# Turning the memory rows with 16 identity columns, partly in 64-wide tiles

## The chip, the cores and the metric

The program runs on one core of a Trainium2 chip. The metric is the device time of one execution in microseconds (us); three executions of the kernel before took 1811.97, 1812.57 and 1812.88 us, so the median is 1812.57. One more execution was taken with the hardware profiler, and every duration below comes from it.

## The reference

The operator joins two independent parts along the last axis. Part A is a long convolution (a shift filter, a product with `v`, an FFT convolution over 2048 positions, a skip term and a product with `q`). Part B is a transformer layer that carries eight memory rows from segment to segment; the change lies in part B:

```python
mem = mem0                                             # 8 rows of 1024
for s in range(n_seg):                                 # 64 segments of 32 rows
    h = concat([mem, x[:, 32*s:32*s+32]], axis=1)      # 40 rows
    q, k, v = (einsum('btd,dhe->bhte', h, W) for W in (Wq, Wk, Wv))   # 32 heads of 128
    p = softmax(where(mask, einsum('bhqe,bhke->bhqk', q, k) * scale, -1e9))
    o = einsum('bhte,hed->btd', einsum('bhqk,bhke->bhqe', p, v), Wo)
    mem = o[:, :8]
    outs.append(o[:, 8:])
```

A segment needs the first eight output rows of the one before it, so the segments follow one another strictly. The weights are bfloat16, 1024 x 4096 for each of q, k and v and 4096 x 1024 for the output.

## The kernel before

The first 437 us or so hold part A and, woven into it, the work of part B that doesn't depend on the memory (the last eight rows of every segment are projected there, and the `x` rows are stored transposed in `REC`). Then come the 64 segments, one after another, in an order written out by hand (`tc.manual_schedule`): each engine runs the instructions in the order of the code, and the framework adds the waits.

**Weights.** The weights are cut into chunks of 128 x 2048 bfloat16 (512 KB). Most stay in SBUF for all segments under names such as `Wres`, `Wmid`, `Wlate`, `Wmore` and `pw`; two are held in spare PSUM columns and copied out in quarters (`quarter`, `quarter_b`; a part of one lies in the second half of `tps`). The other chunks, 14 in a segment, are read again in every segment from a DRAM copy `WS` into `wring`, a ring of five tiles. `fetch()` issues such a load on SP's queue as soon as `done()` has released a tile, that is, when the last matmul that reads it is through.

**A segment.** `rec` is loaded by a POOL DMA; its first 256 columns are `hT`, the segment's input transposed: eight blocks of 128 input features by 32 rows, of which columns 0 to 7 are the memory rows and 8 to 31 `x` rows. `Proj.run` (L941) multiplies one block of `hT`, a 128 x 32 stationary operand, with a chunk: four matmuls, one for each 32 columns of the array (`tile_position=(0, 32 * c)`), each with 512 moving columns. The order of the projections is k0, q0, k1, q1, v0, v1, with transposes, scores, softmax and attention between them. The output projection (`out_half`, L1032) has the attention output as a stationary operand 64 columns wide, so two matmuls of 256 moving columns stand side by side (`tile_position=(0, 64 * dh)`). It accumulates the output features in four quarters, two for each `yacc[f]`, f = 0 and 1. ScalarE copies `yacc[f]` to `Y` (L1121): rows 0 to 39 hold the 40 output rows for the features of the first half, rows 64 to 103 those of the second half.

**The memory rows.** `fill_mem(hT, Y, half)` brings the eight memory rows from `Y` into columns 0 to 7 of the next segment's `hT`. For each of its two 128-column blocks of `Y`, `turn_tile` (L885) transposes the block in four matmuls with the identity as the moving operand (128 columns, `is_transpose`), each writing 32 rows of the bfloat16 PSUM tile `tps`. Then one VectorE copy (L894) takes the wanted 32 values of each partition, 8 of every 64 columns, to `hT`. `turn_tile` also serves the transposes of k0 and q0, which don't change.

**Where it is called.** Half 0 needs only the features of `yacc[0]`. It is called inside the output projection of f = 1, before the fourth of its five last chunks (L1113 and L1114), so that its copy runs beside the chunks that follow. Half 1 needs `yacc[1]`; it is called in the next segment after the first four steps of k0 (L1055), followed by two steps of q0 and then by the steps of k0 that read it. The first segment calls both on `mem0` (L1052, L1055); the last one doesn't call half 0.

Of the kernel before, what the change touches and what calls it, by code (L numbers as in the profile page):

```python
# [10 lines left out]
F32 = mybir.dt.float32  # L11
# [411 lines left out]
def b_kernel(ctx: ExitStack, tc, x, mem0, Wq, Wk, Wv, Wo, outb, n_seg, run_a):  # L423
    nc = tc.nc
    SEG = 32
    NX = 24
    NM = 8
# [47 lines left out]
    ident = const.tile([128, 128], BF, name="ident")  # L475
# [263 lines left out]
    with c0p:  # L739
# [16 lines left out]
        for g in range(2):  # L756
# [3 lines left out]
            for tb in range(4):  # L760
                vst = vsts[:, tb] if g == 0 else pair()[:].rearrange("p (c w) -> p c w", c=4)
                for c in range(4):
                    ps = ps0.tile([128, 512], F32, tag="ps0", name="vb_ps")
                    for kc in range(8):
                        v_last = nc.tensor.matmul(ps[:], lhsT=xbt(kc)[:, 16 * tb:16 * tb + 16, :].rearrange("p s t -> p (s t)"),  # L765
                                                  rhs=ws[kc][:, c * 512:(c + 1) * 512], start=(kc == 0), stop=(kc == 7))
# [21 lines left out]
    tps = ps_t.tile([128, 2, 512], BF, name="tps")  # L788
# [89 lines left out]
    pend = {}  # L878
# [6 lines left out]
    def turn_tile(dst, src):  # L885
        for e in range(0, 128, 32):
            nc.tensor.matmul(dst[e:e + 32, :], lhsT=src[:, e:e + 32], rhs=ident[:], start=True, stop=True,  # L887
                             is_transpose=True, tile_position=(0, e))

    def fill_mem(hT, Y, half):  # L890
        tp = tps[:, 0, :]
        for j in (2 * half, 2 * half + 1):
            turn_tile(tp[:, j * 128:(j + 1) * 128], Y[:, j * 128:(j + 1) * 128])
        nc.vector.tensor_copy(  # L894
            hT.rearrange("p (dh j) t -> p dh j t", dh=2)[:, :, 2 * half:2 * half + 2, 0:NM],
            tp.rearrange("p (j dh r) -> p dh j r", j=4, dh=2)[:, :, 2 * half:2 * half + 2, 0:NM])

    with tc.manual_schedule():
        for _ in range(RING - 2):
# [2 lines left out]
        Y = one.tile([128, 512], BF, tag="PT", name="Y0")  # L902
# [3 lines left out]
        with tc.issue_after(v_last.ins):  # L906
            nc.tensor.matmul(SB[:, 0:320], lhsT=ident[:], rhs=P_pad[:].rearrange("p b k -> p (b k)"), start=True, stop=True,
                             skip_group_check=True)
# [7 lines left out]
        for s in range(n_seg):  # L916
            now[0] = s
            last = s + 1 == n_seg
            hT, KBs, QBs = pend.pop(s)
# [116 lines left out]
            def out_half(hp, f, OT, stop=False):  # L1036
                w = pieces((3, hp, 0))
                for hh in range(2):
                    project(2 * hp + hh, f, w, OT, stop and hh == 1)
                if f == 1:  # L1040
                    done((3, hp, 0))
# [6 lines left out]
            def out_quarter(ch, q, w):  # L1048
                project(2 * ch[1] + q // 2, q % 2, w, OT1)

            if s == 0:
                fill_mem(hT, Y, 0)  # L1052
            k0 = Proj(0, 0).run(4)
            q0 = Proj(1, 0)
            fill_mem(hT, Y, 1)  # L1055
            q0.run(2)
            k0 = k0.run(4).evac()
# [52 lines left out]
            Y = one.tile([128, 512], BF, tag="PT", name="Y")  # L1110
            for f, hps in enumerate((LAST, LAST[-1:] + LAST[:-1])):
                for n, hp in enumerate(hps):
                    if f == 1 and n == 3 and not last:  # L1113
                        fill_mem(pend[s + 1][0], Y, 0)  # L1114
                    out_half(hp, f, OT1, n == 4)
                    for step in steps.get((f, n), ()):
                        if len(step) == 2:
                            out_quarter(KEPT_A if step[0] == "A" else KEPT_B, step[1], qs.pop(step))
                        else:
                            qs[step[:2]] = (quarter if step[0] == "A" else quarter_b)(*step[1:])  # L1120
                nc.scalar.copy(Y[:, 256 * f:256 * f + 256], yacc[f][:, 0:256])  # L1121
# [6 lines left out]
def kernel(  # L1128
# [27 lines left out]
    with ExitStack() as ctx_b:  # L1156
        b_kernel(ctx_b, tc, B_x[0], B_mem0[0],
                 B_Wq.rearrange("d h e -> d (h e)"), B_Wk.rearrange("d h e -> d (h e)"),
                 B_Wv.rearrange("d h e -> d (h e)"), B_Wo.rearrange("h e d -> (h e) d"),
                 outb, n_seg, run_a)  # L1160
# [35 lines left out]
```

## Time and profile before

| | |
|---|---|
| median of three executions | 1812.57 us |
| the profiled execution | 1807.46 us |
| its span, first to last instruction | 1805.7 us |
| TensorE (PE) busy | 1700.6 us, 94% |
| weight loads (PEld) busy | 999.9 us, 55% |
| VectorE (DVE) busy | 1035.2 us, 57% |
| ScalarE (ACT) busy | 658.6 us, 36% |
| HBM traffic | 344 GB/s over the span |

The span is the time from the first to the last instruction that the profiler saw; the execution's own time is 1.8 us longer. A row of a timeline gives the start in us, the duration, the engine, the line, the operation and its tiles (`out<-in`), and how many instructions were joined (x8 is eight). TensorE's matmuls overlap: four matmuls on different 32-column tiles run side by side, and a matmul's duration includes its way through the array, so what a group of matmuls costs is read from start to start and not from durations. A row of the chain of work is start, time on the chain, and the engine with its line. In a group's row the numbers after the bar are busy us, mean ns of one instruction, and idle us of the engine just before them with what ended it. In the view of waits a row is total us, number of waits and the longest.

### The profile page before, as it was taken

The numbers are of one execution on the slowest core, as the hardware profiler recorded it, in microseconds if no ns is written. First come the engines' busy times: TensorE is split into PE (matmuls) and PEld (weight loads), VectorE is DVE, ScalarE is ACT, GpSimd is POOL, SyncE is SP. The second block draws the span as 40 slices with busy tenths as digits, with TensorE's granted clock in tenths as the row PEclk, the third lists the DMA queues.
The fourth block names the chain that finished last, engine by engine and source line by source line (L and its number), as shares of the span: only waits on it lengthen the run. The fifth ranks groups of instructions, "written<-read, shape, count | busy, mean of one in ns | idle before, by whom it ended". The sixth has DMA issues, their size and how long they took to land.

```text
span 1805.7 us, 71361 instructions
## 1 busy us (share of the span) xinstructions
PE 1700.6 (94%) x30996; PEld 999.9 (55%) x31028; DVE 1035.2 (57%) x3429; ACT 658.6 (36%) x1157; POOL 266.1 (15%) x499
## 2 busy tenths in 40 slices
PE   6889997697899999999999999999999999999998
PEld 3443333243566666666666666666666656666665
DVE  9926885433455555555556555555555555555555
ACT  6954650001233333333333333333333333333333
POOL 4002342100111111111111111111111111111111
PEclk9999998799999999999999999999999999999999
DMA  9989988999999999999999999999999999999997
GB/s 344 358 316 293 307 276 274 317 314 309 335 353 367 356 360 351 360 361 361 363 353 365 358 358 370 361 356 358 362 351 363 364 347 363 363 363 364 357 364 294
DMA packets 233071, 623.35 MB, mean 345 GB/s; under 512 B 72802, under 2 KB 72946, under 8 KB 232756
## 3 DMA queue, kind: packets, MB, share of 16 engines
q1 hardware_dynamic: 160948, 550.58, 82.8%
q0 software_dynamic: 17056, 45.13, 7.1%
q10 hardware_dynamic: 54752, 23.07, 4.8%
q8 instruction: 243, 3.98, 0.9%
q14 instruction: 72, 0.59, 0.1%
HBM read 563.63 MB, written 57.67 MB: 344 GB/s over the span
## 4 chain that ended last, share of the span: by engine, by line
PE 76%; DMA 10%; DVE 7%; ACT 4%; issue 3%; ACTq 1%; POOL 0%; SPq 0%; POOLq 0%; DVEq 0%
PE acc L941 32%; PE yacc L1032 23%; DMA wring<-WS 5%; PE kb_ps L624 4%; PE tps L887 3%; PE vb_ps L765 2%; PE tps L960 2%; ACT OT L1022 2%; DVE mx L975 2%; DVE E L977 2%; PE s_ps L247 1%; DMA REC<-stage 1%; DMA out_dram<-ot 1%; ACT s_sb L249 1%; PE ks_ps L285 1%
## 5 line engine op out<-in xcount | busy, mean ns | idle before, releaser
L1032 PEld LDWEIGHTS <-OT 128*64 128x64 bf16 x8255 | 439.3, 109 | 58.4 <-ACT OT L1022 37.1
L941 PEld LDWEIGHTS <-rec 128*32 128x32 bf16 x12288 | 288.4, 96 | 266.6 <-DVE rec L894 36.5
L950 ACT CAST qkv_sb<-acc 128x512 bf16<-128x512 f32 x384 | 225.1, 586 | 511.7 <-PE acc L941 506.0
L941 PE MATMUL acc<-Wres,rec 128*32 128x512 bf16 x3328 | 238.8, 380 | 1.8 <-issue 1.8
L941 PE MATMUL acc<-wring,rec 128*32 128x512 bf16 x2300 | 226.9, 381 | 6.6 <-DMA wring<-WS 5.5
L1032 PE MATMUL yacc<-Wmore,OT 128*64 128x256 bf16 (+1 forms) x2560 | 220.1, 274 | 0.0
L941 PE MATMUL acc<-Wmid,rec 128*32 128x512 bf16 x3072 | 211.7, 379 | 1.7 <-issue 1.7
L1032 PE MATMUL yacc<-wring,OT 128*64 128x256 bf16 x2448 | 195.9, 274 | 6.6 <-DMA wring<-WS 6.6
L1121 ACT CAST Y<-yacc 128x256 bf16<-128x256 f32 x128 | 47.7, 373 | 274.1 <-DVE quarter_b L797 168.1
L941 PE MATMUL acc<-pw,rec 128*32 128x512 bf16 x1796 | 142.9, 380 | 1.1 <-issue 1.0
L797 DVE TENSOR_SCALAR quarter<-OTp 128x256 int32<-128x256 int32 x252 | 99.6, 416 | 73.2 <-ACT OT L1022 73.2
L1022 ACT CAST OT<-OTp 128x640 bf16<-128x640 f32 x128 | 87.5, 683 | 138.3 <-PE OTp L1014 138.2
L1123 POOL DMA_DIRECT2D out_dram<-Y x128 | 63.7, 502 | 499.9 <-ACT Y L1121 499.8
L894 DVE COPY rec<-tps 128x32 bf16<-128x32 bf16 x128 | 22.3, 174 | 173.5 <-PE tps L887 173.5
L941 PE MATMUL acc<-Wlate,rec 128*32 128x512 bf16 x1536 | 116.7, 379 | 0.2 <-issue 0.2
L1060 DVE COPY KT<-tps 128x512 bf16<-128x512 bf16 x64 | 27.2, 425 | 152.6 <-PE tps L887 152.6
L975 DVE TENSOR_REDUCE mx<-SB 128x8 f32<-128x320 f32 x128 | 62.9, 492 | 71.0 <-PE SB L969 71.0
L882 POOL DMA_DIRECT2D rec<-REC x64 | 36.3, 567 | 443.9 <-PE acc L941 428.3
L980 ACT ACTIVATE E<-E 128x320 f32<-128x320 f32 x128 | 60.1, 469 | 77.8 <-DVE E L977 77.8
L1032 PE MATMUL yacc<-Wlate,OT 128*64 128x256 bf16 x1024 | 78.8, 276 | 6.0
L624 PE MATMUL kb_ps<-XBT,pw 128*128 128x512 bf16 x314 | 80.6, 394 | 2.5 <-DMA pw<-in_B_Wk_dram 1.4
L925 POOL COPY KT<-rec 128x128 bf16<-128x128 bf16 x128 | 38.4, 300 | 261.6 <-PE SB L969 257.6
(222 smaller groups left out, 2629.4 us busy)
## 6 DMA issues: line engine op xcount, KB each, us to landing
wring<-WS SPq DMA_DIRECT2D x831, 512.0 KB, 6.0
wring<-WS SPq DMA_DIRECT2D x64, 384.0 KB, 5.3
rec<-REC POOLq DMA_DIRECT2D x64, 192.0 KB, 5.6
SK<-s_sb SPq DMA_DIRECT2D x16, 512.0 KB, 5.3
SU<-s_sb SPq DMA_DIRECT2D x16, 512.0 KB, 4.9
Kg<-SK SPq DMA_DIRECT2D x32, 256.0 KB, 4.1
Ug<-SU SPq DMA_DIRECT2D x32, 256.0 KB, 5.4
REC<-stage ACTq DMA_DIRECT2D x16, 512.0 KB, 13.3
```

Source lines behind the costliest of these rows:

```text
L624: nc.tensor.matmul(ps[:], lhsT=ws[kc][:, hl * 128:(hl + 1) * 128], rhs=xbt(kc).rearrange("p s t -> p (s t)"), start=(kc == 0), stop=(kc == 7))
L797: nc.vector.tensor_scalar(out=dst, in0=src, scalar1=0, scalar2=None, op0=ALU.bitwise_or)
L887: nc.tensor.matmul(dst[e:e + 32, :], lhsT=src[:, e:e + 32], rhs=ident[:], start=True, stop=True, is_transpose=True, tile_position=(0, e))
L925: nc.gpsimd.tensor_copy(KT[:, :, :, 32:40], KBs[:, 128 * g:128 * g + 128].rearrange("p (c i t) -> p i c t", c=4, i=4))
L941: nc.tensor.matmul(self.acc[32 * c:32 * c + 32, :], lhsT=hT[:, ch[1], :], rhs=w[:, 512 * c:512 * c + 512], start=(ch == chs[0]), stop=(ch ...
L950: nc.scalar.copy(sb[:], self.acc[:])
L975: nc.vector.tensor_reduce(out=mx[:], in_=S, op=ALU.max, axis=AX.X)
L980: nc.scalar.activation(E[:], E[:], ACT.Exp, scale=scale)
L1022: nc.scalar.copy(OT[:], o_view)
L1032: nc.tensor.matmul(yacc[f][64 * dh:64 * dh + m, x - o:y - o], lhsT=lhsT, rhs=r, start=(h == (0, 2 * FIRST[-1])[f] and x == o), stop=stop, ...
L1121: nc.scalar.copy(Y[:, 256 * f:256 * f + 256], yacc[f][:, 0:256])
L1123: nc.gpsimd.dma_start(bass.AP(outb.tensor, outb.offset + SEG * s * 2048 + 512 * dh, [[2048, 32], [1, 512]]), Y[64 * dh + NM:64 * dh + 40, :])
```

## The change

The turned rows are computed by ordinary matmuls with float32 output in place of transposes. The moving operand is no longer the whole identity but `mem_cols`, its columns 0 to 7 and 64 to 71, so a matmul has 16 moving columns and yields just the eight memory rows of both feature halves. The output lies in the first 64 float32 columns of what was the transposes' half of `tps`; half 0 uses columns 0 to 31 and half 1 columns 32 to 63. The copy reads contiguous float32 in place of every eighth stretch of bfloat16. `fill_mem` gets a width: 32 as before, in two rounds of four matmuls, or 64, in two rounds of two. The call inside the output projection passes 64; the calls beside the projections keep 32. Over the program TensorE gets 252 fewer matmuls and 252 fewer weight loads; the orders of the other engines and the waits are the same.

```diff
-    def fill_mem(hT, Y, half):
-        tp = tps[:, 0, :]
+    mem_cols = ident[:].rearrange("p (dh x) -> p dh x", dh=2)[:, :, 0:NM]
+
+    def fill_mem(hT, Y, half, wide=32):
+        tp = tps[:, 0, 0:128].bitcast(F32)
         for j in (2 * half, 2 * half + 1):
-            turn_tile(tp[:, j * 128:(j + 1) * 128], Y[:, j * 128:(j + 1) * 128])
+            for e in range(0, 128, wide):
+                nc.tensor.matmul(tp[e:e + wide, 16 * j:16 * j + 16], lhsT=Y[:, j * 128 + e:j * 128 + e + wide], rhs=mem_cols,
+                                 start=True, stop=True, skip_group_check=True, tile_position=(0, e))
         nc.vector.tensor_copy(
             hT.rearrange("p (dh j) t -> p dh j t", dh=2)[:, :, 2 * half:2 * half + 2, 0:NM],
-            tp.rearrange("p (j dh r) -> p dh j r", j=4, dh=2)[:, :, 2 * half:2 * half + 2, 0:NM])
+            tp.rearrange("p (j dh r) -> p dh j r", j=4, dh=2)[:, :, 2 * half:2 * half + 2, :])
...
-                        fill_mem(pend[s + 1][0], Y, 0)
+                        fill_mem(pend[s + 1][0], Y, 0, 64)
```

## The prediction

> **What bounds the kernel now.** I read the page first, then the windows of the steady part, the chain of work, the DMA view, the waits, and last the instructions around the two places that the change touches. From the page, what the DMAs moved in its forty slices of 45 us (the 64 segments begin in the tenth):
>
> ```profile
> GB/s 344 358 316 293 307 276 274 317 314 309 335 353 367 356 360 351 360 361 361 363 353 365 358 358 370 361 356 358 362 351 363 364 347 363 363 363 364 357 364 294
> ```
>
> Windows of the part with the 64 segments (us, PE, PEld, DVE, ACT, POOL busy; then granted clock, DMA share, GB/s):
>
> ```profile
> 900.00:1000.00 100.00, 98.44 (x2134) 62.87 (x2129) 58.63 (x222) 36.06 (x67) 11.63 (x26) 1.00 0.98 358
> ...
> 1600.00:1700.00 100.00, 99.47 (x2193) 63.97 (x2185) 57.40 (x221) 35.92 (x67) 13.15 (x29) 1.00 0.99 365
> ```
>
> TensorE is busy 98 to 99% at the full granted clock, and the 16 DMA engines are busy 98 to 99% in the same windows. Two resources are full at once, so the question is which one sets the length of a segment. The chain shows one `tps` group of eight matmuls of 0.23 us per segment (`fill_mem` inside the output projection); their starts are a clock for the segments:
>
> ```profile
> 512.16 0.23 PE tps L887 x8
> ...
> 1591.34 0.23 PE tps L887 x8
> 1612.19 0.23 PE tps L887 x8
> ...
> 1695.55 0.23 PE tps L887 x8
> ...
> 1758.56 0.23 PE tps L887 x8
> ```
>
> The five segments from 1591.34 to 1695.55 take 104.21 / 5 = 20.84 us each, and so does 1591.34 to 1612.19. That is the floor that TensorE sets when nothing makes it wait. Not all are so short. The first and last row enclose 59 segments: 1246.40 / 59 = 21.13 us on average, 0.29 us over the floor, 16.8 us in all. Counted by the starts of the 60 VectorE copies that follow these fills, 25 of the 59 lie within 0.03 us of the floor. What ends the extra time, in the waits of the steady part:
>
> ```profile
> PEld L941 <- issue: 17.9, 31, 1.3
> ...
> PE acc L941 <- DMA wring<-WS: 3.8, 8, 0.9
> ```
>
> The second row names the streamed weights. The first has no named releaser, but it stands before the same projections and its 31 waits of 0.58 us on average have the size of the segments' excess; I read it as the same cause. The DMA view of the steady part shows how close the stream is:
>
> ```profile
> DMA packets 132006, 460.39 MB, mean 360 GB/s; under 512 B 17419, under 2 KB 17419, under 8 KB 131733
> ```
>
> ```profile
> wring<-WS SPq DMA_DIRECT2D x788, 512.0 KB, 6.0
> wring<-WS SPq DMA_DIRECT2D x60, 384.0 KB, 5.3
> ```
>
> 848 loads in 1280 us are one in 1.51 us, each 6.0 us under way: 6.0 / 1.51 = 4.0 of the ring's five tiles are in flight at any time. TensorE has about one loaded tile in hand. So it is the nominal bound, with the weight stream right behind it.
>
> **The change part by part.** The place in the output projection (`fill_mem(..., 0)`) and the place after the first four projection steps (`fill_mem(..., 1)`), TensorE's starts in a floor segment:
>
> ```profile
> 1653.37 0.39 PE L1032 MATMUL yacc<-Wmore,OT 128*64 128x256 bf16 x4
> 1653.59 0.27 PE L1032 MATMUL yacc<-B_rest,OT 128*64 128x256 bf16 x2
> 1653.65 0.22 PE L1032 MATMUL yacc<-quarter_b,OT 128*64 128x128 bf16 x1
> 1653.80 0.29 PE L887 MATMUL tps<-ident,Y 128*32 128x128 bf16 x8
> 1654.03 0.41 PE L1032 MATMUL yacc<-Wring,OT 128*64 128x256 bf16 x4
> 1654.27 0.39 PE L1032 MATMUL yacc<-pw,OT 128*64 128x256 bf16 x4
> 1654.58 0.40 PE L941 MATMUL acc<-wring,rec 128*32 128x512 bf16 x4
> 1654.81 0.82 PE L941 MATMUL acc<-Wlate,rec 128*32 128x512 bf16 x12
> 1655.46 0.28 PE L887 MATMUL tps<-ident,Y 128*32 128x128 bf16 x8
> 1655.57 0.60 PE L941 MATMUL acc<-Wmid,rec 128*32 128x512 bf16 x8
> 1656.02 0.40 PE L941 MATMUL acc<-wring,rec 128*32 128x512 bf16 x4
> ```
>
> *Half 0, in the output projection.* From the start of the `quarter_b` matmul to that of `pw` pass 1654.27 - 1653.65 = 0.62 us. Without the fill these would be a half-width step (1653.59 to 1653.65, 0.06) and four `Wring` matmuls (as 1653.37 to 1653.59, 0.22): 0.28. The fill costs 0.34 us, three times the 0.11 that the same eight matmuls cost at 1655.46, where the neighbours are 32 columns wide as they are. The difference stands in the gaps to 64-wide neighbours: 1653.71 to 1653.80 before it, and as much after it. The change removes both switches and leaves four 64-wide matmuls of 16 moving columns, two rounds of two.
>
> *Price of a round.* No row of before has 16 columns. The nearest is the score matmul with 40, four tiles side by side:
>
> ```profile
> 1660.49 0.27 PE L966 MATMUL SB<-KT,QT 128*32 128x40 bf16 x16
> 1660.59 0.24 PE L969 MATMUL SB<-KT,rec 128*32 128x160 bf16 x4
> ```
>
> Sixteen in 0.10 us, with their sixteen weight loads, are 0.025 a round; 1660.59 is rounded, so I take 0.027. The upper end is the 64-wide round as it runs now, 0.22 / 2 = 0.11, in which the loads are hidden behind 256 columns. I take 0.027, since both are rounds of few columns, and keep 0.11 for the range. Half 0 then costs 0.054 in place of 0.34: 0.286 saved, at worst 0.12. Times 63 segments: 18.0 us (7.6).
>
> *Half 1, beside the projections.* Two rounds of 0.027 in place of the 0.11 between 1655.46 and 1655.57: 0.056 saved, at worst nothing. Times 64: 3.6 us (0). The call ahead of the first segment happens once and counts nothing.
>
> The Trainium skill ("TensorE: Matmul & The Clock Gate", LDWEIGHTS) lets a weight load take its columns over 1.2 per ns, so by an estimate from it 64 columns take 53 ns and a half-0 round 0.053 us; half 0 would then save 0.234, and the predicted time below would be 1805.1. The 0.025 of the 32-wide rounds fits that rule; no row of before shows 64-wide loads without cover.
>
> *The copies.* Both fills end in a VectorE copy, now out of float32 PSUM:
>
> ```profile
> L894 DVE COPY rec<-tps 128x32 bf16<-128x32 bf16 x128 | 22.3, 174 | 173.5 <-PE tps L887 173.5
> L1060 DVE COPY KT<-tps 128x512 bf16<-128x512 bf16 x64 | 27.2, 425 | 152.6 <-PE tps L887 152.6
> L975 DVE TENSOR_REDUCE mx<-SB 128x8 f32<-128x320 f32 x128 | 62.9, 492 | 71.0 <-PE SB L969 71.0
> L966 PE MATMUL SB<-KT,QT 128*32 128x40 bf16 x2048 | 35.2, 180 | 1.1 <-issue 1.1
> ```
>
> ```profile
> 1654.20 0.17 DVE L894 COPY rec<-tps 128x32 bf16<-128x32 bf16 x1 [1.27 <-PE tps L887]
> 1655.79 0.17 DVE L894 COPY rec<-tps 128x32 bf16<-128x32 bf16 x1 [1.42 <-PE tps L887]
> ```
>
> bfloat16 costs (425 - 174) / 480 = 0.52 ns an element over a base of 157 ns; float32, by the reduction, (492 - 157) / 320 = 1.05. So 32 elements take 191 ns, 17 more. Against that the last matmul of a fill ends sooner (180 ns at 40 columns, 0.22 us at 128). In half 1 the copy does end the wait: it is done at 1655.97 and the next load's matmul starts at 1656.02, about 0.02 us after the eight `Wmid` matmuls would let it. Forty ns less and 17 more leave that as it is: nothing, give or take 0.02. In half 0 the copy is done at 1654.37 and `acc` starts at 1654.58, so it is covered by eight output matmuls (0.44) and the switch back to 32-wide tiles (0.09). After the change, counted from the fill's start at 1653.71, the copy is through near 1654.27 and TensorE near 1654.29. It stays covered by 0.02; without the cover the segment would lose just that remainder.
>
> *The rest.* 252 fewer matmuls and weight loads; no DMA, queue or wait on another engine is moved, and the DVE, ACT, POOL and SP orders are the same. Each reissue of the ring comes as much sooner as TensorE does, which is where the DMA side comes in.
>
> *Sum.* TensorE's floor falls by 18.0 + 3.6 = 21.6 us, 0.34 us a segment (bound below: 7.6). How much of it arrives? A segment without a wait gains it whole; one that already waits for weights comes to the wait sooner and waits longer. 25 of 59 segments had no wait: 21.6 x 25 / 59 = 9.1 us. This is a choice between ends that lie far apart, nothing and 21.6. The rows are for the middle: a floor of 20.50 would need 360 x 21.13 / 20.50 = 371 GB/s, and the slices of the page reach 370 only once, but 363 to 365 often. The profiled execution took 1807.46 us in all; it would become 1798.4. It lies 5.1 below the median of the runs, and the same step from 1812.57 gives **1803.5**.
>
> **The rivals.**
> - *All of it arrives* (the waits have other causes than the stream's rate, or it speeds up when asked sooner): 1812.57 - 21.6 = 1791.0. For it: 25 floor segments, and 365 GB/s in the best window. Against it: 0.98 to 0.99 DMA share, four of five tiles in flight.
> - *The stream sets the pace and nothing arrives*: 1812.6, or 1810 if a tenth does. For it: with a share of 0.98 there is little idle DMA time to use. The Trainium skill ("DMA: Bandwidth & Descriptors", Where 436 GB/s comes from) has HBM give one core about 358 GB/s; by that rule the 360 of the steady part are the end, and the time would stay. Windows at 365 and a slice at 370 speak against a hard end there.
> - *Slower: the weight loads come out of cover.* If each round waits for a load and then runs, a round costs what these rows say plus 0.027:
>
> ```profile
> L1032 PEld LDWEIGHTS <-OT 128*64 128x64 bf16 x7743 | 414.1, 110 | 58.4 <-ACT OT L1022 37.1 <-issue 7.5
> L941 PEld LDWEIGHTS <-rec 128*32 128x32 bf16 x12288 | 288.4, 96 | 266.6 <-DVE rec L894 36.5 <-issue 20.2
> ```
>
> Half 0 is then 2 x 0.137 = 0.27, half 1 2 x 0.123 = 0.25, together 0.52 against 0.45 now: 63 x 0.07 = 4.4 us, 1817.0. It decides from 0.113 us a round. The score matmuls at 0.025 with loads as short-lived speak against it.
>
> **How the numbers follow.** No change means within 0.2% (3.6 us), about what a measurement of this kernel can tell. Part of the gain, 4 to 15 us: 0.56. All of it: 0.12. Nothing: 0.22. Slower: 0.10. Of the first case 0.04 may fall within 0.2%, and of the nothing case 0.02 beyond it on the faster side and 0.01 on the slower: faster 0.52 + 0.12 + 0.02 = 0.66, same 0.04 + 0.19 = 0.23, slower 0.11. The range leaves out most of the full gain and of the slower case: 1794 to 1814; the likeliest case alone spans 1797.6 to 1808.6.
>
> **What would show it.** Right: the fill in the output projection has four matmuls with about 0.05 us to the next `yacc` matmul and no gap around it; floor segments of about 20.5; a higher GB/s in the steady windows; more or longer waits of `acc` and `yacc` for `wring`, and in the chain a larger share for the DMA. Wrong: floor segments still near 20.8 (price of a round), segments at 20.5 throughout (full gain), or an average that stays at 21.1 with a lower floor (the stream).

## The result and the profile after

The changed kernel took 1799.43 us (median; 1796.39 to 1800.37) beside 1812.72 for the kernel before: 13.3 us less, a ratio of 0.9919 with a 95% interval of 0.9894 to 0.9944. A second set of executions gave 1800.94 beside 1811.51: 10.6 us less, 0.9947 (0.9924 to 0.9969). Forecast were 1803.5 and a step of 9.1 us.

The profiled execution of the changed kernel took 1800.37 us, 0.9 over its median; that of before took 1807.46, 5.3 under its own. So the two profiles show only 7.1 us between them, and the floors and waits below are compared with this in mind.

TensorE's starts in a floor segment of the changed kernel (start, duration, engine and line, operation, tiles, count; L896 is the line of the new matmuls):

```profile
1501.64 0.27 PE L1036 MATMUL yacc<-B_rest,OT 128*64 128x256 bf16 x2
1501.70 0.22 PE L1036 MATMUL yacc<-quarter_b,OT 128*64 128x128 bf16 x1
1501.75 0.21 PE L896 MATMUL tps<-ident,Y 128*64 128x16 bf16 x4
1501.81 0.39 PE L1036 MATMUL yacc<-Wring,OT 128*64 128x256 bf16 x4
1502.03 0.39 PE L1036 MATMUL yacc<-pw,OT 128*64 128x256 bf16 x4
1502.35 0.40 PE L945 MATMUL acc<-wring,rec 128*32 128x512 bf16 x4
1502.58 0.82 PE L945 MATMUL acc<-Wlate,rec 128*32 128x512 bf16 x12
1503.22 0.21 PE L896 MATMUL tps<-ident,Y 128*32 128x16 bf16 x8
1503.28 0.60 PE L945 MATMUL acc<-Wmid,rec 128*32 128x512 bf16 x8
1503.77 0.40 PE L945 MATMUL acc<-wring,rec 128*32 128x512 bf16 x4
```

The gaps around half 0 are gone: 1501.70 to 1502.03 is 0.33 us, where it was 0.62. The four 64-wide matmuls take 1501.75 to 1501.81, 0.03 a round. In half 1 the eight matmuls take 0.06 in place of 0.11.

The starts of half 0 in the chain of work, three segments in a row, and the two VectorE copies of the first and the last half 0 of the steady part, 59 segments apart:

```profile
1522.74 0.04 PE tps L896 x4
...
1543.27 0.04 PE tps L896 x4
...
1563.80 0.04 PE tps L896 x4
```

```profile
512.96 0.19 DVE L898 CAST rec<-tps 128x32 bf16<-128x32 f32 x1 [1.07 <-PE tps L896]
...
1752.32 0.19 DVE L898 CAST rec<-tps 128x32 bf16<-128x32 f32 x1 [1.07 <-PE tps L896]
```

The floor is 20.53 us (20.84 before), the mean (1752.32 - 512.96) / 59 = 21.01 (21.13 before). The floor fell by 0.31, and the excess over it rose from 0.29 to 0.48: 13 of the 59 segments lie within 0.03 us of the floor, where 25 did before. The waits of the steady part (total, number, longest) say where:

```profile
PEld L945 <- issue: 25.0, 48, 1.4
...
PE acc L945 <- DMA wring<-WS: 8.9, 20, 1.1
...
PE acc L945 <- issue: 4.5, 12, 0.9
```

The first row had 17.9 us before and the second 3.8; the third had 4.7. The steady window (PE, PEld, DVE, ACT, POOL busy; granted clock, DMA share, GB/s) shows a stream that is as full as it was:

```profile
500.00:1780.00 1280.00, 1257.38 (x27619) 800.50 (x27615) 728.84 (x2744) 459.61 (x853) 163.87 (x366) 1.00 0.98 362
```

So three questions were put to the chip: which part of the change made the floor, whether the stream's rate holds back the rest, and what the waits without a releaser are.

### The profile page after: what moved, and what is told of

Its sections match the earlier page's. It is cut to its first block, busy times and chain, and to the rows that moved or that the text cites. A ratio compares the mean times of both kernels' runs of the same rounds, so it can differ in the third digit from the quotient of the medians.

```text
span 1798.6 us, 70857 instructions
## 1 busy us (share of the span) xinstructions
PE 1690.5 (94%) x30744; PEld 995.1 (55%) x30776; DVE 1037.2 (58%) x3429; ACT 658.8 (37%) x1157; POOL 265.7 (15%) x499
## 4 chain that ended last, share of the span: by engine, by line
PE 73%; DMA 13%; DVE 6%; ACT 5%; issue 3%; ACTq 1%; POOL 0%; SPq 0%; POOLq 0%; DVEq 0%
PE acc L945 32%; PE yacc L1036 21%; DMA wring<-WS 8%; PE kb_ps L624 5%; PE vb_ps L765 2%; PE tps L964 2%; ACT OT L1026 2%; PE tps L887 2%; DVE E L981 1%; DVE mx L979 1%; ACT s_sb L249 1%; DMA REC<-stage 1%; PE s_ps L247 1%; DMA VBD<-pair 1%; PE ks_ps L285 1%
## 5 line engine op out<-in xcount | busy, mean ns | idle before, releaser
L898 DVE CAST rec<-tps 128x32 bf16<-128x32 f32 x128 | 24.5, 191 | 157.6 <-PE tps L896 153.6
```

## The experiments

Each kernel was timed beside the kernel before. "Floor" is the length of an undisturbed segment, read in each trace as above; two rows of the chain are rounded each, so their difference can be 0.01 off the table.

### Which part of the change makes the floor

`e1_cols_only`: the changed kernel without the switch of width, so 16 columns in 32-wide tiles at both places.

```diff
-                        fill_mem(pend[s + 1][0], Y, 0, 64)
+                        fill_mem(pend[s + 1][0], Y, 0)
```

> The changed kernel, but with 32-wide tiles in the output projection too: 16 columns and float32 output everywhere, and the two switches of tile width stay. Theory (the switches are the larger part of the fill's price): two rounds of 0.027 in place of 0.054 save about 0.05 us in half 0 and about 0.02 in half 1, so floor segments of 20.77 us in place of 20.84 and 1808 to 1812 us. Rival (the 112 columns that are not streamed carry the gain): floor near 20.53 and 1799 us.

`e2_wide_only`: the kernel before, its half 0 in 64-wide tiles with all 128 identity columns and float32 output; half 1 as it was.

```diff
-                        fill_mem(pend[s + 1][0], Y, 0)
+                        fill_wide(pend[s + 1][0], Y)    # for j, e: matmul(tp[e:e+64, 128*j:...+128], lhsT=Y[:, ...64], rhs=ident)
```

> The kernel before with one edit: in the output projection four matmuls 64 wide with all 128 identity columns and float32 output; half 1 stays the old transposes. Theory: the switches go and two rounds of 0.054 stay, so half 0 costs 0.11 in place of 0.34 us, floor segments of 20.61 and 1802 to 1807 us. Rival (columns carry the gain): floor near 20.84, 1812 us.

`e3_half0_only`: the kernel before with the new half 0 (16 columns, 64-wide), half 1 as it was.

```diff
-                        fill_mem(pend[s + 1][0], Y, 0)
+                        fill_new(pend[s + 1][0], Y, 0, 64)
```

> The kernel before with the new 64-wide 16-column fill in the output projection alone; half 1 stays the old transposes. Theory: nearly the whole gain, floor 20.55 and 1798 to 1802 us, as half 1 saves 0.11 - 0.054 in the matmuls and loses most of it again to its copy, which ends the wait of the next projection step. Rival (the prediction's term for half 1 holds): floor 20.59 and 2 us slower than the changed kernel.

`e4_after_again`: the changed kernel itself, on the same chip as these three.

> The changed kernel itself beside the others on the same chip: 1797 to 1801 us, 11 to 15 us under the kernel before.

Two half-0 fills in a row from the chain of e1, of e2 and of e3:

```profile
1099.57 0.15 PE tps L896 x8
...
1120.31 0.15 PE tps L896 x8
```

```profile
1206.36 0.11 PE tps L902 x4
...
1226.97 0.11 PE tps L902 x4
```

```profile
1014.74 0.04 PE tps L904 x4
...
1035.31 0.04 PE tps L904 x4
```

| kernel | floor, us | against before | median, us | ratio (95%) |
|---|---|---|---|---|
| before | 20.84 | | 1811.51 | |
| e1, columns alone | 20.73 | -0.10 | 1808.97 | 0.9986 (0.9969 to 1.0003) |
| e2, width alone (half 0) | 20.61 | -0.23 | 1802.63 | 0.9953 (0.9931 to 0.9974) |
| e3, half 0 whole | 20.56 | -0.28 | 1801.91 | 0.9937 (0.9913 to 0.9961) |
| e4, the whole change | 20.53 | -0.31 | 1800.94 | 0.9947 (0.9924 to 0.9969) |

The larger part is the switch of tile width: without it (e1) two thirds of the floor's gain are missing, and the time can't be told from before. Going 64, 32, 64 columns costs 20.73 - 20.53 = 0.20 us a segment, 0.10 a switch. The Trainium skill ("TensorEngine Tiling (Array Packing)", Key Properties) says that a change of the tiling mode drains TensorE; the price of 0.10 us a switch agrees with that, though the traces do not show what TensorE does in this time. Half 1 brings 0.03 (e3 against e4), less than the 0.056 forecast. The medians of e2, e3 and e4 lie within each other's intervals, so only their floors order them.

### Does the stream's rate hold back the rest?

`e5_light_before` and `e6_light_after`: two of the 14 streamed chunks of a segment aren't loaded, and a resident chunk stands in for them; TensorE's instructions stay the same, but the output is not the operator's.

```diff
+    DROP = (ORDER[19], ORDER[58])    # never fetched
...
     def pieces(ch):
+        ch = STAND_IN.get(ch, ch)    # a resident chunk
```

> The kernel before with two of the 14 streamed chunks of each segment no longer loaded (their matmuls read a resident chunk instead, so those two chunks' weights are wrong and the output is not the reference's): about 1 MB of 7.5 MB less in each segment, TensorE's instructions the same. Theory (the segments' time over the floor is the weight stream): nearly every segment at the floor of 20.84 us, so about 17 us less, 1794 to 1798 us. Rival (the excess has another cause): 1810 to 1813 us.

> The changed kernel with the same two chunks no longer loaded (output not the reference's). Theory: every segment at the new floor of 20.53, so the whole 63 x 0.31 = 19.5 us under the light kernel before, 1774 to 1779 us. Rival (the part of the gain that is missing is lost to something other than the stream): 13 us under the light kernel before, as without the edit.

`e7_heavy_before` and `e8_heavy_after`: the one streamed chunk of which a quarter is resident is loaded whole, 128 KB more in every segment.

```diff
-    nc.sync.dma_start(t[:, 512:2048], stream_src(ch)[:, 512:2048])
+    nc.sync.dma_start(t[:], stream_src(ch))
```

> The kernel before with one load made heavier: the chunk of which 384 KB are loaded in each segment is loaded whole, 128 KB more that nothing reads, 1.7% more bytes. Theory: more waits for weights, 1817 to 1826 us, floor segments of 20.84 rarer. Rival (the stream has room): 1813 us.

> The changed kernel with the same heavier load. Theory: the stream takes a larger part of the gain, so 3 to 9 us under the heavy kernel before, not 13. Rival: 13 us under it, as without the edit.

| stream | before, us | after, us | gain | of a floor gain of |
|---|---|---|---|---|
| light (e5, e6) | 1794.39 | 1777.20 | 17.2 | 19.6 |
| as it is (before, e4) | 1811.51 | 1800.94 | 10.6 | 19.3 |
| heavy (e7, e8) | 1816.14 | 1801.72 | 14.4 | 19.6 |

The floor gain is the floors' difference (0.306 to 0.311 us) times 63. The ratios' intervals leave each gain some 4 to 5 us either way. With the light stream the measured gain is consistent with all of it; with the stream as it is, it is not (the first reading, 13.3 us, leaves at most 19.2). But the two gains, 17.2 and 10.6, differ by about as much as their uncertainties together, and 17.2 can't be told from the 13.3 of the first reading. That a lighter stream lets more of the floor's gain through is likely, and not shown. The heavy pair contradicts its expectation of a smaller gain: 128 KB in each of the 60 such loads of the steady part are 7.9 MB, which at the 360 GB/s of before would be 22 us if the stream set the pace. They cost 4.7 us before the change (e7 stayed a little under the 1817 expected at the least) and 0.8 after it, and the stream ran faster. The steady windows of e7 and of e8 (columns as above):

```profile
500.00:1740.00 1240.00, 1219.92 (x26652) 772.80 (x26642) 697.53 (x2627) 440.07 (x817) 156.82 (x349) 1.00 0.98 363
```

```profile
500.00:1740.00 1240.00, 1216.45 (x26725) 776.35 (x26721) 706.02 (x2655) 444.93 (x826) 158.97 (x354) 1.00 0.99 368
```

368 GB/s held over 1240 us. By the Trainium skill's per-core figure of about 358 (cited in the prediction) that could not be, so the trace disagrees. The Trainium skill's page "Perfetto Trace Analysis" (Roofline) lets a single active core pull more than that share, and with this the trace agrees.

The steady window of e5, and then the waits of e5 and of e6, with the light stream:

```profile
500.00:1740.00 1240.00, 1230.85 (x27074) 781.58 (x27070) 706.78 (x2665) 445.28 (x828) 159.54 (x356) 1.00 0.92 314
```

```profile
PEld L947 <- issue: 4.0, 10, 1.1
...
PE acc L947 <- issue: 0.9, 2, 0.6
```

```profile
PEld L951 <- issue: 14.4, 17, 2.0
...
PE acc L951 <- issue: 7.6, 12, 1.5
```

In neither is there a row of a projection that waits for `wring`: with 314 GB/s wanted, the stream is never late. Yet the waits without a releaser are still there, in e6 as large as in the kernel before. They can't be late weights. (The two profiles are single executions, e5's the fastest of 6 and e6's the slowest of 5, so the difference between them is not the change's.)

### What the waits without a releaser are

`e12_before_again` is the kernel before, profiled once more and timed as a second reading of it.

> The kernel before itself, for a second profiled execution of it. Theory A (the waits ahead of a weight load that no semaphore ends come at every 256th TensorE instruction, where the next block of instructions is fetched, and their total varies between executions): floor 20.84 again, those waits anywhere between 12 and 25 us, each about 1.3 to 1.7 us after an instruction fetch landed. Theory B (they are waits for streamed weights, as the prediction read them): each within 0.2 us after a ring load landed.

It took 1812.40 beside 1811.62 (ratio 1.0005, 0.9988 to 1.0021). One such wait in its timelines, on TensorE and on its weight loads:

```profile
982.62 0.39 PE L941 MATMUL acc<-wring,rec 128*32 128x512 bf16 x4
982.84 0.38 PE L941 MATMUL acc<-pw,rec 128*32 128x512 bf16 x2
...
983.93 0.82 PE L941 MATMUL acc<-pw,rec 128*32 128x512 bf16 x10 [0.71 <-issue]
```

```profile
983.92 0.33 PEld L941 LDWEIGHTS <-rec 128*32 128x32 bf16 x10 [1.20 <-issue]
```

The step stops after two of its four matmuls, and its operands are `pw`, which is resident, and `rec`, which it has been reading: there is no data to wait for. Windows cut at ten late starts of TensorE (the second and third columns of figures are PE and PEld, with their counts). Eight of them are such waits; at 906.68 a step breaks for 0.1 us, and the one at 913.38 is put down to half 0's copy, but lasts 0.60 where 0.20 is usual:

```profile
900.70:906.68 5.98, 5.83 (x127) 3.36 (x128) 4.93 (x22) 2.81 (x5) 0.57 (x1) 1.00 0.99 335
906.68:913.38 6.70, 6.41 (x131) 5.59 (x127) 3.36 (x14) 1.31 (x3) 0.00 (x0) 1.00 0.96 345
913.38:924.30 10.92, 10.88 (x255) 5.25 (x256) 5.05 (x20) 4.17 (x9) 2.12 (x5) 1.00 1.00 363
924.30:966.14 41.84, 41.52 (x901) 26.24 (x894) 23.83 (x90) 14.90 (x29) 5.37 (x12) 1.00 0.98 361
966.14:983.89 17.75, 16.96 (x384) 11.27 (x383) 8.93 (x31) 5.38 (x10) 2.69 (x6) 1.00 0.96 356
983.89:1008.84 24.95, 24.39 (x511) 14.79 (x511) 14.80 (x59) 9.75 (x18) 2.69 (x6) 1.00 0.97 352
1008.84:1026.70 17.86, 17.09 (x383) 11.55 (x383) 8.11 (x31) 5.37 (x10) 2.39 (x5) 1.00 0.98 353
1026.70:1051.19 24.49, 23.44 (x511) 14.41 (x511) 14.94 (x56) 9.09 (x18) 2.99 (x7) 1.00 0.98 353
1051.19:1057.66 6.47, 5.93 (x127) 3.14 (x128) 4.83 (x22) 2.81 (x5) 0.56 (x1) 1.00 0.88 300
```

128, 127, 256, 894, 383, 511, 383, 511 and 128 weight loads lie between them: within two of one, one, two, seven, three, four, three, four and one times 128. With the matmul that belongs to each load these are multiples of 256 instructions.

The same count can be made without choosing the places: TensorE's matmuls and weight loads are numbered through a trace, and those weight loads of the steady part are taken that stood idle 0.5 us or more with no releaser. "On the grain" are those whose numbers agree modulo 256, to within one.

| one execution of | such waits, us | on the grain, us |
|---|---|---|
| before | 16, 14.5 | 12, 11.3 |
| before again (e12) | 17, 15.9 | 13, 12.3 |
| after | 26, 19.0 | 17, 13.3 |
| light before (e5) | 4, 3.2 | 4, 3.2 |
| light after (e6) | 13, 13.2 | 13, 13.2 |

So in the kernel before these waits are mostly on the grain, and in the changed kernel a third of them are not. With the light stream all are on it, so the others go with the weight stream: the row without a releaser holds two kinds of wait.

The DMA view of the steady part of the same run has a queue of that grain (packets, MB, share), and its window has the count of the instructions:

```profile
q8 instruction: 210, 3.44, 1.1%
```

```profile
500.00:1740.00 1240.00, 1222.34 (x26759) 776.67 (x26751) 700.23 (x2641) 440.59 (x820) 156.45 (x349) 1.00 0.98 359
```

210 packets of 16 KB for 53,510 matmuls and weight loads: one for every 255. In the trace TensorE goes on 1.2 to 1.75 us after one of these packets has landed. So the waits on the grain are TensorE running out of instructions, because their next block is late. The Trainium skill ("Runtime: NRT & Kernel Launch", Instruction fetch mechanics) has an engine's instructions come in blocks of 16 KiB, 256 instructions, by a DMA queue of its own; the trace agrees. The Trainium skill also says there that the rate of issue hides the fetch, and here it is not always hidden: in e12 13 of the 210 blocks cost 0.5 us or more. Why a block is late stays open. The busy DMA engines have a part in when it lands: from the last landing to the instruction that begins a new block pass 1.9 to 2.1 us in the median in the two traces of before and the two of after, and 2.6 in e5 and e6. But e6, at a DMA share of 0.93, lost as much to late blocks as the others (13.2 us in the table), and the packets of late blocks took 1.0 to 1.1 us in the median, like the rest.

Put to their causes over the whole steady part, from the traces: a TensorE step's delay over the median of its place in the segment counts as "load" when a ring load landed in the 0.2 us before, and as "fetch" when an instruction block had landed 1.2 to 1.75 us before. Part of a delay is caught up later in the segment, so the sums exceed the segments' excess. The sums are rough: a ring load lands every 1.5 us and an instruction block every 5.9, so some delays fall to either by chance, and other limits for what counts as a delay move single entries by up to 5 us.

| one execution of | load, us | fetch, us | other, us |
|---|---|---|---|
| before | 5.9 | 12.4 | 2.3 |
| before again (e12) | 5.5 | 16.8 | 3.7 |
| after | 12.6 | 18.2 | 3.8 |
| after again (e4) | 14.2 | 23.1 | 5.7 |
| light before (e5) | 0 | 4.9 | 1.0 |
| light after (e6) | 0 | 15.6 | 2.9 |
| heavy before (e7) | 5.9 | 21.2 | 3.7 |
| heavy after (e8) | 11.5 | 19.8 | 3.2 |

Late loads went up by 6 to 9 us in each pair in which there are any (by 4 to 8 with other limits), and this is the steadier half of the missing gain. The fetch waits go up by 6 us in both readings of the stream as it is and by 11 with the light one, but down by 1 with the heavy one, and they differ by 4 to 5 between two executions of one kernel; their share of the loss is less certain.

### Is there more to be had beside the copies?

`e9_late_fill`: half 0's fill one chunk later, so that one chunk less covers its copy.

```diff
-                    if f == 1 and n == 3 and not last:
+                    if f == 1 and n == 4 and not last:
```

> The changed kernel with the fill of the output projection one chunk later, so that four output matmuls (0.22 us) stand behind it in place of eight. Theory (its VectorE copy was covered with little to spare): the next segment's first projection step waits for the copy, 0.1 to 0.2 us more in every floor segment (20.63 to 20.73), 1802 to 1809 us. Rival (the copy has ample cover): no change from the changed kernel, 1799 us.

`e10_third_q0_step`: a third step of q0 between half 1's fill and the first step of k0 that reads it, taken from the four q0 steps that follow k0 (the weights are fetched in the new order).

```diff
-    q0.run(2) ... q0.run(4) ... q0.run(2).evac()
+    q0.run(3) ... q0.run(3) ... q0.run(2).evac()
```

> The changed kernel with a third step of q0 (one that needs only half 0) moved between half 1's fill and the steps of k0 that read it; the streamed chunks and their number stay, one is read 0.22 us later. Theory (half 1's copy still ends a wait of about 0.05 us): floor 0.04 to 0.06 lower, 20.48, and 1 to 3 us less than the changed kernel. Rival (that wait is hidden or the stream takes it all): the same time as the changed kernel.

`e11_q0_step_mended`: the same, but four steps stay behind k0 and one is left for the end.

```diff
-    q0.run(2) ... q0.run(4) ... q0.run(2).evac()
+    q0.run(3) ... q0.run(4) ... q0.run(1).evac()
```

> The third q0 step ahead of the reading steps of k0, as before, but with the steps of q0 split 3, 4 and 1 in place of 3, 3 and 2, so that four steps again stand between k0's evacuation and its transposes. Theory (the run without that lost 0.2 us a segment there, waiting for ScalarE's evacuation, and did gain 0.05 at half 1's copy): floor 0.04 to 0.06 under the changed kernel, 20.48 us, and 0 to 4 us less time. Rival (the third step itself costs, wherever the evacuation stands): floor above 20.55 and no gain.

Half 0 of two segments in a row in the chain of e9 and of e11, and the waits of the weight loads for k0's evacuation and for the two copies of a segment in the changed kernel, in e10 and in e11:

```profile
893.10 0.06 PE tps L896 x4
...
913.80 0.06 PE tps L896 x4
```

```profile
1018.37 0.04 PE tps L896 x4
...
1038.84 0.04 PE tps L896 x4
```

```profile
PEld L887 <- ACT qkv_sb L954: 39.6, 107, 0.7
PEld L945 <- DVE rec L898: 37.4, 117, 1.4
```

```profile
PEld L887 <- ACT qkv_sb L954: 51.1, 112, 0.7
...
PEld L945 <- DVE rec L898: 21.8, 116, 0.7
```

```profile
PEld L887 <- ACT qkv_sb L954: 40.2, 109, 0.7
...
PEld L945 <- DVE rec L898: 24.5, 115, 1.6
```

e9: floor 20.70, time 1804.95 (ratio 0.9956, 0.9938 to 0.9974). A fill 0.22 us later, by a chunk's step, costs 0.17, so about 0.05 of the cover had been to spare. e10: floor 20.67, 1805.58 (0.9957, 0.9944 to 0.9971). The waits for the copies fall from 37.4 to 21.8 us (those for half 1's alone from 21.7 to 9.2), but k0's evacuation by ScalarE, which four q0 steps had covered, shows now: 39.6 to 51.1, and the floor is worse by 0.14, where 0.05 less was expected. e11 gives that cover back: floor 20.46, 0.07 under the changed kernel, and 1800.39 beside 1811.62 (0.9944, 0.9923 to 0.9964). Its time can't be told from that of the changed kernel: 0.07 x 63 = 4.5 us of floor, of which a part arrives, lie within the intervals. No version tried here beats the changed kernel by more than the measurement is uncertain.

## Why the prediction was right, and where it was not

*Half 0.* Right: 0.29 us saved a segment, 0.286 forecast. Both gaps went with the switch of width, and a round costs 0.03 (taken: 0.027), though it has 64-wide loads; the score matmuls were the right row to go by. The prediction's estimate of 0.053 us a round, from the Trainium skill's rule for weight loads, does not agree with the trace; whether the loads are shorter or run beside each other is not shown. (By the prediction's own sum that estimate gives 1804.8 us, not 1805.1.)

*Half 1.* The fill shrank as forecast, from 0.11 to 0.06, but the segment gained only 0.03 (e3 against e4) of 0.056. The step that failed is "nothing, give or take 0.02" for the copy's wait: after 1503.28 the eight `Wmid` matmuls need 0.43, as those of before did with their 0.02 of idle time (0.45 - 0.02), and the next step starts at 1503.77, so the wait is 0.06. TensorE reaches it 0.05 us sooner, but the copy ends at 1503.71, 0.49 after the fill's start, where it was 0.50 (1655.96 less 1655.46). The rows are rounded; in the median of the steady part it is 0.484 after 0.512, so the copy comes 0.028 us sooner where TensorE comes 0.05 sooner, and the rest goes into the wait. What the prediction took as unchanged is the time between the fill's last matmul and the copy: that matmul ends 0.208 us after the fill's start where it was 0.285, but the copy starts at 0.293 where it was 0.337 (medians again), 0.085 behind the matmul's end where it was 0.05. Why this time grew is not shown. The copy itself grew as forecast, 174 to 191 ns:

```profile
1503.52 0.19 DVE L898 CAST rec<-tps 128x32 bf16<-128x32 f32 x1 [1.27 <-PE tps L896]
```

```profile
L898 DVE CAST rec<-tps 128x32 bf16<-128x32 f32 x128 | 24.5, 191 | 157.6 <-PE tps L896 153.6 <-DMA rec<-REC 4.0
```

*Half 0's copy.* Covered, as forecast; the margin is nearer 0.05 us (e9) than 0.02.

*The floor.* 0.31 us a segment, 19.5 us over 63, where 0.34 and 21.6 were forecast.

*The share that arrives.* 13.3 and 10.6 of 19.5 us, 0.68 and 0.54, where 25/59 = 0.42 was taken. The time came out 4.1 us under the forecast: the larger share gave 0.26 x 19.5 = 5.1 more, the smaller floor 0.42 x 2.1 = 0.9 less. The intervals leave the share at 0.52 to 0.98 by the first reading and 0.29 to 0.71 by the second, so the term was too low by the first and cannot be faulted by the second. Why waiting segments gain as well is not shown; that only undisturbed ones gain was a rule without a row. That the time fell into the range is in part luck: the range of 1794 to 1814 holds any share up to 0.86.

*The cause of the waits.* Wrong, and this is the step that failed: "I read it as the same cause". The row with no releaser, 17.9 of the 21.7 us that the two quoted rows of before give, is mostly instruction blocks, not weights: of its 31 waits 22 lie on the grain, 13.2 of the 17.9 us. The row named no releaser, and one was read into it. With it falls the argument on the share that a floor of 20.50 would need 371 GB/s: 368 were to be had (e8).

*The rivals.* "All of it arrives" did not happen with the stream as it is (0.98 at most), and may have, within the uncertainty, with the light one. "The stream sets the pace" is refuted by the gain and by the heavy pair. "Slower" would have needed 0.113 us a round; it is 0.03.

## What to carry to other kernels

Price a small foreign group in a stream of matmuls from start to start of its neighbours: here the two switches of tile width were two thirds of what the change took off the floor, the columns and all else one third. Before a wait "by issue" is put down to the data, count the instructions between such waits: whole multiples of 256 pointed to the instruction stream here. And when work is moved to cover one wait, look for the wait that it covered before (e10).

## What was not expected of the hardware

TensorE at 98 to 99% busy still lost more than 11 us of 1240 waiting for its own instructions (the waits on the grain before, those of 0.5 us and more alone), one 16 KB block for every 255, and resumed 1.2 to 1.75 us after the block had landed. And 16 DMA engines that looked full at 360 GB/s gave 368 when more was asked of them.
